# A fifth load buffer, fewer key-value products and a new order in a retention and feed-forward kernel

## The chip, the cores and the metric

The kernel runs on one core of a Trainium2 chip. The metric is the device time of one execution in microseconds (us); less is better. The time of a kernel is the median of several runs.

## The reference

The inputs are `q`, `k` and `v` of shape (8, 8, 576, 64): 8 batches, 8 heads, 576 tokens, 64 elements. First comes a causal retention (attention without a softmax, with a decay for each head), then a feed-forward layer on the 4608 tokens with their heads side by side.

```python
scores = scale * np.matmul(q, k.transpose(0, 1, 3, 2))
gamma = 1.0 - 2.0 ** (-5.0 - np.arange(H, dtype=np.float32))
rel = pos[:, None] - pos[None, :]
Dmat = np.where(rel >= 0, gamma[:, None, None] ** rel[None, :, :], 0.0)
attn = np.matmul(scores * Dmat[None, :, :, :], v)
x = attn.transpose(0, 2, 1, 3).reshape(B * S, H * D)      # 4608 x 512
h = x @ w_in                                              # 512 x 2048
out = np.maximum(0.01 * h, h) @ w_out                     # 2048 x 512, fp32 out
```

## The kernel before

**Units.** The 4608 tokens go in 36 units of 128 (`u`), each two halves of 64 tokens (`j`). A batch has 576 / 64 = 9 halves (`CB`), so batches begin and end in the middle of units. The ninth half of a batch is its last: `live(u, j)` is false there, since no later token of the batch needs its key-value state; `fresh(u, j)` marks a batch's first half.

**Retention of a unit.** `load` (L856) brings k, q and v as fp32, one buffer each from a ring (`ld_pool`, `CFG["ld"]` deep). `casts` (L883) turns k into fp16 (`ck`) and q and v into fp16 with their decay (`cq`, `cv`). q and k are turned around by TensorE (`turn_pe`, units 0 to 7) or by a transposing DMA on SyncE's queue (`turn_dma`, later). `inner` (L962) computes with 64x64 matmuls the scores of each half (`sa`, L973) and the key-value products of each half (`sb`, L982), both into one PSUM tile; VectorE masks the scores (`mk`, L988) and adds the products to the running fp32 state (`st`, L1031 to L1038; tile `s32`), which is cast to fp16 (`sx`, L1051 and L1054; tile `st16`). `outer_mm` (L1092) multiplies scores with values and states with queries (L1096), and `outer_copy` (L1140) copies the outcome into `xT`, the feed-forward layer's input. From unit 13 on the small matmuls of a unit are one burst (`bu`); for units 4 to 11 they are three parts (`sb`, `ca`, `ow`).

**Feed-forward.** Groups of 512 tokens (`g`, nine of them). Groups 0 to 2 use a plain first layer (`layer1`, L1201); groups 3 to 8 use seven products instead of eight on 2x2 blocks (`layer1_set`, L1382), with sums of blocks made by VectorE; the second layer does so in all groups (`layer2`, L1465). ScalarE applies the activation (L1208, L1405, L1414); copies of PSUM between products (`cA`, `u2`, `k5`) run on ScalarE or VectorE, as a list says.

**The order.** Nothing is scheduled by the compiler. Every step is a job with an engine, a modelled cost, what it comes after, and the buffers that it opens and uses. `Plan.order` (L121) plays the jobs through: each engine takes, of the jobs that can start within a slack, the one with the least latest start. That comes from due times of the main stages, the modelled costs of what follows, and two tables of corrections for single jobs, `nudge` and `shift_due`. A third table, `eng`, with five strings of letters for the default, says which engine does a step. The instructions of each engine are then written in the order found. DMAs are modelled as two servers, SyncE's and GpSimd's. GpSimd issues the loads of units 0 to 11 and of both weights in one fixed order, in the same queue as its own casts and scalings; SyncE issues the loads of later units, the transposes and the stores.

**Fillers.** Where the plan shows a gap on TensorE of some length ahead of 60 us, `filler` (L1559) puts matmuls of a zeroed tile there (L1574); `fill_tight` is the time until which short gaps are filled too.

Of the kernel before, what the change touches and what calls it, by code (L numbers as in the profile page):

```python
# [9 lines left out]
FP = mybir.dt.float32  # L10
F16 = mybir.dt.float16
# [36 lines left out]
class Plan:  # L48
# [72 lines left out]
    def order(self, margin=30, slack=30, filler=None):  # L121
# [57 lines left out]
        while todo:  # L179
# [76 lines left out]
def _cfg():  # L256
# [40 lines left out]
    nudge = {  # L297
        -125060:
            "b1.p2.1 ",
        -12876:  # L300
            "so3.1 ",
        -129001:
            "b1.p4.1 ",
        -135715:
            "b1.21 ",
        -137832:
            "b1.11 ",
        -149466:
            "b2.p4.1 ",
        -1547:  # L310
            "mk25 ",
        -15631:
            "b3.p5.0 ",
        -15982:
            "mk27 ",
        -166028:
            "m3.3.0 ",
        -168918:
            "tp5.1 ",
        -18270:  # L320
            "a7.0.p7.0 ",
        -19132:
            "bu32 ",
        -224663:
            "wm1.1 ",
        -2292:
            "m5.2.1 ",
        -239388:
            "wm0.1 ",
        -23999:  # L330
            "b4.p6.1 ",
        -241662:
            "ws3.1 ",
        -25911:
            "ck33 ",
        -2823:
            "b3.p7.1 ",
        -283444:
            "h1.8.256 ",
        -284183:  # L340
            "b0.11 ",
        -289278:
            "ws3.0 ",
        -291604:
            "h1.10.256 ",
        -292799:
            "h1.4.256 ",
        -292880:
            "h1.14.256 ",
        -293315:  # L350
            "b1.p1.1 ",
        -295060:
            "h2.12.0 ",
        -296205:
            "m0.2.0 ",
        -296904:
            "h1.0.0 ",
        -296915:
            "h1.2.0 ",
        -297398:  # L360
            "wm3.1 ",
        -298104:
            "h1.6.0 ",
        -298106:
            "h1.4.0 ",
        -298370:
            "h1.2.256 ",
        -298539:
            "m0.0.1 ",
        -299439:  # L370
            "tp3.1 ",
# [1312 lines left out]
```

## Time and profile before

| | |
|---|---|
| median of 3 runs | 288.48 us (288.45 to 289.79) |
| the profiled execution | 286.13 us, span 284.1 us |
| granted TensorE clock | 0.999 |
| busy, of the span | TensorE 274.5, VectorE 221.9, ScalarE 182.2, GpSimd 92.9 us |
| HBM | read 36.81 MB, written 9.44 MB |
| DMA | 50.06 MB, mean 176 GB/s |

The span is from the first to the last instruction of the profiled execution; the time of the whole execution lies 2.0 us above it. In lines of the profile PE is TensorE's matmuls, PEld its weight loads, DVE VectorE, ACT ScalarE, POOL GpSimd, SP SyncE, and a trailing q the engine's queue. `L982` is line 982 of the kernel. A group's row has the engine, the instruction, out<-in, the shape and count, then the busy time in us, the mean of one in ns, and after a bar the idle time ahead of it with what ended it. Matmuls overlap in the array, so the duration of one is longer than the step from one to the next.

### The profile page before, as it was taken

How to read it: one execution, taken by the hardware profiler on the slowest of the kernel's cores; microseconds unless marked ns; L12 is line 12 of the kernel's file. 1: busy time of each engine (PE TensorE's matmuls, PEld its weight loads, DVE VectorE, ACT ScalarE, POOL GpSimd, SP SyncE). 2: the span in 40 equal slices, each digit the busy share in tenths (PEclk: the TensorE clock that was granted, in tenths of full speed). 3: DMA queues.
4: the chain of work that ended last, by engine and by line, in shares of the span. 5: the costliest groups of instructions: out<-in, count | busy, mean ns of one | idle time of the engine just before them, and what ended most of it. 6: DMA issues, size and time to landing. Idle time of an engine off the chain costs nothing.

```text
span 284.1 us, 10441 instructions
## 1 busy us (share of the span) xinstructions
PE 274.5 (97%) x4530; PEld 231.8 (82%) x4530; DVE 221.9 (78%) x394; ACT 182.2 (64%) x373; POOL 92.9 (33%) x109
## 2 busy tenths in 40 slices
PE   8989899999999999999999999999999999999994
PEld 3668787887788888888888878888888888888883
DVE  3775899865888699898969889889897876955762
ACT  2366576676579598768767766877656755755720
POOL 8888987910122311337324134522100000000000
PEclk9999999999999999999999999999999999999999
DMA  7999999999999999999999999990312002100304
GB/s 158 290 262 237 275 183 284 320 217 228 273 234 194 226 231 272 202 225 240 225 224 212 230 215 229 248 229 0 76 47 105 2 2 76 75 0 3 148 2 148
DMA packets 118797, 50.06 MB, mean 176 GB/s; under 512 B 107488, under 2 KB 112224, under 8 KB 118752
## 3 DMA queue, kind: packets, MB, share of 16 engines
q1 hardware_dynamic: 110368, 35.82, 55.6%
q0 software_dynamic: 7056, 13.11, 19.2%
q8 instruction: 35, 0.57, 0.8%
q10 hardware_dynamic: 1328, 0.47, 0.6%
q14 instruction: 10, 0.08, 0.1%
HBM read 36.81 MB, written 9.44 MB: 163 GB/s over the span
## 4 chain that ended last, share of the span: by engine, by line
PE 82%; DVE 7%; DMA 5%; issue 2%; POOL 2%; ACT 0%; DVEq 0%; POOLq 0%; ACTq 0%
PE acc L1465 38%; PE acc L1382 26%; PE acc L1201 10%; PE ot L1096 4%; DMA w_in<-in_moe_w_in_dram 3%; DMA qkT<-qk 2%; PE sc L982 2%; PE sc L973 2%; POOL t L865 1%; DVE mix L1441 1%; DVE sum L1409 1%; PE acc L938 1%; DVE v L896 1%; DVE s L1037 1%; DVE s L988 1%
## 5 line engine op out<-in xcount | busy, mean ns | idle before, releaser
L1465 PEld LDWEIGHTS <-gt 128*128 128x128 f16 x720 | 69.6, 98 | 8.9 <-ACT gt L1405 0.3
L1465 PE MATMUL acc<-w_out,gt 128*128 128x256 f16 x432 | 54.4, 273 | 0.1
L1201 PE MATMUL acc<-xT,w_in 128*128 128x128 f16 (+1 forms) x512 | 47.1, 246 | 0.5 <-issue 0.5
L1201 PEld LDWEIGHTS <-w_in 128*128 128x128 f16 x512 | 39.1, 98 | 4.4 <-issue 0.7
L1382 PEld LDWEIGHTS <-w_in 128*128 128x128 f16 x384 | 36.8, 98 | 5.5 <-issue 0.8
L1414 ACT ACTIVATE gt<-sum 128x512 f16<-128x512 f32 x48 | 29.8, 629 | 17.8 <-DVE sum L1409 17.7
L1208 ACT ACTIVATE gt<-acc 128x512 f16<-128x512 f32 x48 | 27.8, 594 | 19.9 <-PE acc L1201 19.7
L1405 ACT ACTIVATE gt<-acc 128x512 f16<-128x512 f32 x48 | 28.6, 595 | 14.5 <-PE acc L1382 14.0
L896 POOL TENSOR_TENSOR qk<-t,cs 128x512 f16<-128x512 f32 x19 | 20.6, 1090 | 50.7 <-PE sc L982 22.1
L1465 PE MATMUL acc<-w_mix,gt 128*128 128x256 f16 x288 | 36.4, 273 | 0.0
L1465 PEld LDWEIGHTS <-mix 128*128 128x128 f16 x288 | 27.7, 98 | 4.0 <-DVE mix L1441 0.5
L1382 PEld LDWEIGHTS <-w_sum 128*128 128x128 f16 x288 | 27.6, 98 | 3.9 <-DVE xs L1362 0.4
L1382 PE MATMUL acc<-xs,w_in 128*128 128x256 f16 x192 | 28.8, 273 | 0.7 <-DVE sum L1409 0.7
L1382 PE MATMUL acc<-xs,w_sum 128*128 128x256 f16 x192 | 28.8, 273 | 0.1
L1382 PE MATMUL acc<-xT,w_in 128*128 128x256 f16 x192 | 28.8, 272 | 0.0
L896 POOL TENSOR_TENSOR v<-t,cs 128x512 f16<-128x512 f32 x18 | 20.3, 1127 | 23.7 <-PE ot L1096 19.5
L988 DVE TENSOR_TENSOR s<-sc,cs 128x512 f16<-128x512 f32 x36 | 24.6, 682 | 1.4 <-PE sc L973 1.4
L1335 ACT COPY k<-acc 128x512 f32<-128x512 f32 x27 | 15.9, 591 | 14.2 <-PE acc L1382 7.9
L1409 DVE TENSOR_TENSOR sum<-acc,k 128x512 f32<-128x512 f32 x24 | 16.5, 689 | 7.8 <-ACT k L1335 4.1
L1033 DVE TENSOR_TENSOR s<-sc,s 128x256 f32<-128x256 f32 x40 | 16.7, 418 | 4.1 <-PE sc L982 3.4
L1327 ACT COPY acc<-acc 128x512 f32<-128x512 f32 x30 | 17.4, 579 | 3.1 <-PE acc L1465 1.8
L1096 PE MATMUL ot<-qkT,st 64*64 64x64 f16 x512 | 17.1, 198 | 1.7 <-ACT st L1051 0.5
(68 smaller groups left out, 463.0 us busy)
## 6 DMA issues: line engine op xcount, KB each, us to landing
out_dram<-osb SPq DMA_DIRECT2D x17, 512.0 KB, 4.1
t<-in_k_dram SPq DMA_DIRECT2D x22, 256.0 KB, 4.3
t<-in_q_dram SPq DMA_DIRECT2D x21, 256.0 KB, 4.6
t<-in_v_dram SPq DMA_DIRECT2D x21, 256.0 KB, 4.3
t<-in_v_dram POOLq DMA_DIRECT2D x11, 256.0 KB, 5.5
t<-in_k_dram POOLq DMA_DIRECT2D x10, 256.0 KB, 6.9
t<-in_q_dram POOLq DMA_DIRECT2D x10, 256.0 KB, 6.1
w_in<-in_moe_w_in_dram POOLq DMA_DIRECT2D x8, 256.0 KB, 6.9
```

The costliest lines, as they stand in the source:

```text
L896: engine[e].tensor_tensor(out=out, in0=t32[u, 2 * x][:], in1=decay(u, x), op=MUL)
L988: landed[u] = nc.vector.tensor_tensor(out=s[:], in0=a[:, :, 0], in1=mask_sb.unsqueeze(1).unsqueeze(1).to_broadcast([P, 2, NP, CH]), op=MUL,)
L1033: nc.vector.tensor_tensor(out=to, in0=x, in1=before[0][:, before[1]], op=ADD)
L1096: i = nc.tensor.matmul(out=ot[half(oo), (j + u) % 2, slot, c, :], lhsT=lhsT, rhs=rhs, start=(first or parted(u)) and (j, oo) not in seen, ...
L1201: nc.tensor.matmul(out=a[:, n, :], lhsT=w_in16[:, c, (f0 + n) * P : (f0 + n + 1) * P], rhs=x[:, c, t0 : t0 + nt], start=(n == 0 and c == 0 ...
L1208: nc.scalar.activation(out=y[:, f0 : f0 + nf, t0 : t0 + nt], in_=a[:], func=mybir.ActivationFunctionType.Lrelu)
L1327: op("cA", ce, lambda: copies[ce](out=B[:], in_=A[:]), [done["1"]], [B], [A], "1", COST[ce, "seed"])
L1382: nc.tensor.matmul(out=r[:, f, :], lhsT=w[:, c, (2 * n + f) * P : (2 * n + f + 1) * P], rhs=rhs[:, c, :], start=fresh and c == 0 and f == ...
L1405: w = op(what, "ACT", lambda: nc.scalar.activation(out=to(), in_=r[:], func=lr), after, [y], [r], m)
L1409: what, "DVE", lambda: nc.vector.tensor_tensor(out=s[:], in0=r[:], in1=plus[:], op=ADD),
L1414: lambda: nc.scalar.activation(out=to(), in_=s[:], func=lr), [j], [y], [s],
L1465: nc.tensor.matmul(out=r[:, tb, :], lhsT=lhs[n]()[:, f, tb * P : (tb + 1) * P], rhs=rhs[n][:, f, :], start=fresh and i == 0 and k == 0, st ...
```

## The change

Three things in the kernel and its plan. The ring of load buffers goes from four to five, and the fp32 states `s32` get a ring of their own, of two, where they had one of four. `sb` leaves out the products of a half that is not `live`. The planner's model changes in places: the cost of a burst follows from its number of matmuls, transfers of the two DMA servers hold each other up in another way, and the first quarter of the output weights is costed longer; fillers are put into gaps from 300 ns (before 350) and by that rule until 45 us (before 24). With that, the tables `eng`, `nudge` and `shift_due` are made anew, so the order of instructions and the engine of many steps differ throughout. The list of loads, the strings of letters and the stages stay as they were. The tables of corrections are cut here.

```diff
--- before.py
+++ after.py
@@ -228,11 +228,12 @@
                     at = max(at, server["SP"] + 370, server["POOL"] + 650)
                     server["SP"], land = at + j.move, 170
                 elif j.eng == "SP":
-                    both = min(j.move, max(0.0, server["POOL"] - at))
-                    server["SP"] = at + j.move + 0.5 * both
-                    server["POOL"] += 0.6 * both
+                    if server["POOL"] > at:
+                        at = server["POOL"]
+                        server["POOL"] += 0.1 * j.move
+                    server["SP"] = at + j.move
                 else:
-                    server["POOL"] = at + j.move + 0.5 * min(j.move, max(0.0, server["SP"] - at))
+                    server["POOL"] = at + j.move + 0.1 * min(j.move, max(0.0, server["SP"] - at))
                 j.end = server[j.eng] + land
                 if j.land is not None:
                     j.end = j.land
@@ -282,423 +283,378 @@
     ]
     eng = {
         "ACT":
-            "yt0.0 sx0.0 sx0.1 yt2.1 sx2.1 yt3.1 sx3.0 sx3.1 yt4.0 sx6 sx7 cq8 cq11 cv11 sx10 sx11 cq13 sx12 "
-            "cq16 cv17 sx17 cq18 cv18 cq20 sx21 sx28 ",
+            "yt0.1 sx0.0 sx0.1 yt1.1 sx2.0 sx3.1 cq4 cv5 sx5 cv7 sx7 cq8 cv9 cv10 sx12 sx13 cq17 cq18 sx19 "
+            "cq21 sx30 sx31 sx32 ",
         "DVE":
-            "ck0 cq0 cv0 ck1 cv1 x0 yt1.0 sx1.1 sx2.0 ck4 ck5 yt4.1 yt5.0 yt7.1 x7 ck8 x8 x9 x11 cq12 cv12 "
-            "ck13 cq14 cv14 x13 sx15 ck17 sx16 ck18 x16 sx19 ck20 ck21 cq21 cv21 sx20 x20 cv25 sx24 ck30 ck31 "
-            "x28 x29 sx31 ck32 x31 sx33 ck34 cq34 x32 sx34 sx35 x34 x35 b0.11 b0.u2 b1.u2 a3.3.k5 b2.u2 "
-            "a4.2.u2 a4.3.cA b3.u2 a5.1.u2 b5.k5 a7.1.u2 a7.2.u2 a7.3.k5 b6.u2 b6.k5 a8.1.cA a8.2.u2 b7.u2 "
-            "b7.k5 b8.cA b8.u2 b8.k5 ",
+            "cq0 cv1 ck2 ck3 sx3.0 x3 ck5 x4 yt5.0 ck7 yt6.1 yt7.1 x7 x9 x11 cq12 cq13 cv13 cq15 x12 x15 ck19 "
+            "x16 x17 cq20 x19 x21 ck24 cq25 cv25 x23 sx25 ck27 sx27 cq28 cv28 cq30 x28 x29 x35 b0.11 b0.u2 "
+            "b0.k5 b1.cA b1.k5 a3.2.u2 a4.1.u2 a4.1.k5 a4.2.cA a4.2.u2 a5.2.u2 a6.2.u2 a7.0.u2 a7.3.cA "
+            "a7.3.k5 b6.u2 b6.k5 a8.1.cA a8.2.u2 b7.u2 b7.k5 b8.cA b8.u2 ",
         "POOL":
-            "cq2 ck3 sx4 sx5 cv7 cv8 ck9 sx8 cq10 cv10 ck11 sx13 sx14 cq19 sx18 ck23 sx22 ck24 ck25 ck27 cv29 "
-            "cv30 cv32 cv33 cv34 ck35 ",
+            "sx1.1 cv2 cv8 sx9 cq10 ck12 ck15 ck16 cv16 cv17 ck18 cq19 sx18 sx21 ck22 ck25 sx24 ck26 ck28 "
+            "ck29 cq29 cv29 sx28 sx29 ck30 cv30 ck31 cv31 ck32 cv32 cv33 sx33 ck34 ck35 cv35 ",
     }
     nudge = {
...
     shift_due = {
...
     eng, nudge, shift_due = ({n: v for v, ns in d.items() for n in ns.split()} for d in (eng, nudge, shift_due))
     return dict(
         main=main, engines=engines, loads=loads, eng=eng, nudge=nudge, shift_due=shift_due,
         split=lambda u: u < 4,
-        ld=4, ap=4, t0=7000, extra=1300, l_late=3000, margin=120, slack=60, fill_until=60000, fill_tight=24000,
+        ld=5, ap=4, t0=7000, extra=1300, l_late=3000, margin=120, slack=60, fill_until=60000, fill_tight=45000,
         sp_after=2, period=27000, wm_due=45000, ws_due=30000,
         landing={"ld0.1": 4100, "ld0.0": 4800, "ld0.2": 6700, "wi0": 10500}, u2=("DVE", "DVE"), joined=12,
         drain=4, plain1=(2,), plain2=(), chain=True, order="1265734", shift=8000, tail="1526374", lead=-2000,
@@ -772,6 +728,7 @@
     ld_pool = pool("ld", CFG["ld"])
     a_pool = pool("ap", CFG["ap"])
     b_pool = pool("bp", 2)
+    c_pool = pool("cp", 2)
     d_pool = pool("dp", 2)
     e_pool = pool("ep", 3)
     x_pool = pool("xp", 2)
@@ -826,7 +783,6 @@
         ("ACT", "f32"): (537, 680),
     }
     add = plan.add
-    BURST = 562
 
     def by(name, default):
         return CFG["eng"].get(name, default)
@@ -953,6 +909,9 @@
     def fresh(u, j):
         return (2 * u + j) % CB == 0
 
+    def states(u):
+        return 4 * (2 - fresh(u, 0) - fresh(u, 1))
+
     def st_before(u, j):
         return st16[u][:, 0] if j else st16[u - 1][:, 1]
 
@@ -963,7 +922,7 @@
 
         a = Buf(sc_pool, [P, 2, 2, NP, CH], FP, "sc", True, turn=u)
         s = s16[u] = Buf(b_pool, [P, 2, NP, CH], F16, "s16", turn=u)
-        f, h = Buf(a_pool, [P, 2, NP, CH], FP, "s32", turn=u), Buf(a_pool, [P, 2, NP, CH], F16, "st16", turn=u)
+        f, h = Buf(c_pool, [P, 2, NP, CH], FP, "s32", turn=u), Buf(a_pool, [P, 2, NP, CH], F16, "st16", turn=u)
         s32[u], st16[u] = f, h
 
         def sa():
@@ -978,11 +937,13 @@
         def sb():
             for p in range(NP):
                 for j in range(2):
-                    for g in range(2):
+                    for g in range(2 if live(u, j) else 0):
                         nc.tensor.matmul(
                             out=a[half(g), j, 1, p, :], lhsT=qk16[u][half(j), u % 2, 1, 2 * p + g, :],
                             rhs=v16[u][half(j), 2 * p + g, :], start=True, stop=True, skip_group_check=True,
                         )
+
+        lives = 8 * (live(u, 0) + live(u, 1))
 
         def mk():
             landed[u] = nc.vector.tensor_tensor(
@@ -1003,16 +964,18 @@
                 sa()
                 sb()
 
+            pairs = 32 + lives + states(u - 1) + (states(u - 2) if cross is not None else 0)
+            burst = 31 + 8.3 * pairs
             ja = jb = add(
-                f"bu{u}", "PE", (BURST, BURST + 268), all_,
+                f"bu{u}", "PE", (burst, burst + 268), all_,
                 [turned[u, 0], turned[u, 1], cast[u, 1], cast[u, 2], written.get(u - 2)] + after, [a],
                 [qkT[u], qk16[u], v16[u]] + uses + (cross[1] if cross is not None else []), mode="q",
             )
         elif parted(u):
-            jb = add(f"sb{u}", "PE", (147, 376), sb, [cast[u, 1], cast[u, 2]], [a], [qk16[u], v16[u]], mode="q")
+            jb = add(f"sb{u}", "PE", (14 + 8.3 * lives, 243 + 8.3 * lives), sb, [cast[u, 1], cast[u, 2]], [a], [qk16[u], v16[u]], mode="q")
         else:
             ja = add(f"sa{u}", "PE", (147, 376), sa, [turned[u, 0], turned[u, 1]], [a], [qkT[u]], mode="q")
-            jb = add(f"sb{u}", "PE", (147, 376), sb, [cast[u, 1], cast[u, 2]], [a], [qk16[u], v16[u]], mode="q")
+            jb = add(f"sb{u}", "PE", (14 + 8.3 * lives, 243 + 8.3 * lives), sb, [cast[u, 1], cast[u, 2]], [a], [qk16[u], v16[u]], mode="q")
         if not parted(u):
             masked[u] = add(f"mk{u}", "DVE", COST["DVE", "psum"], mk, [ja], [s], [a])
         if u - 2 >= CFG["joined"]:
@@ -1184,7 +1147,7 @@
                 in_=moe_w_out[c * FQ : (c + 1) * FQ, :].rearrange("(c k) f -> k c f", k=P),
             )
 
-        w_out_job[c] = add(f"wo{c}", "POOL", (770, 770), run, move=2600, due=load_due("POOL"))
+        w_out_job[c] = add(f"wo{c}", "POOL", (770, 770), run, move=3400 if c == 0 else 2600, due=load_due("POOL"))
         follow(w_out_job[c])
 
     leaks = {g: [] for g in range(NG)}
@@ -1558,7 +1521,7 @@
 
     def filler(free, t):
         early = t < CFG["fill_tight"]
-        if t - free < (350 if early else 500) or t > CFG["fill_until"]:
+        if t - free < (300 if early else 500) or t > CFG["fill_until"]:
             return None
         a = Buf(acc_pool, [P, 1, TOK], FP, "acc", True)
         if free < WARM:
```

More of the change, by code (lines that the diff above doesn't have):

```diff
@@ L318, in _cfg @@
[L318 to L367, printed above, removed]
@@ new lines, in _cfg @@
+        -338987:
+            "so0.0 ",
+        -34656:
+            "sx3.0 ",
+        -35084:
+            "b4.p5.0 ",
+        -3564:
+            "b2.p1.1 ",
+        -36122:
+            "mk30 ",
+        -36124:
+            "x28 ",
+        -36392:
+            "tp3.0 ",
+        -375040:
+            "wm3.1 ",
+        -40345:
+            "bu29 ",
+        -42864:
+            "x32 ",
+        -44830:
+            "x21 ",
+        -45449:
+            "b8.p1.1 ",
+        -51461:
+            "st20.1 ",
@@ new lines, in _cfg @@
+        17340:
+            "b3.p1.0 ",
+        20148:
+            "ck20 ",
+        23507:
+            "st32.1 ",
+        24613:
+            "st28.1 ",
+        251269:
+            "cv6 ",
+        25933:
+            "oa35 ",
+        26568:
+            "ld8.1 ",
+        29552:
+            "xs5.3 ",
+        2977:
+            "st18.0 ",
+        30156:
+            "bu35 ",
+        32293:
+            "b4.p3.0 ",
+        3550:
+            "ck24 ",
+        42319:
+            "b5.p4.0 ",
```

596 lines of the change are left out of this document (275 added, 321 removed).

## The prediction, made before the change was run

> **What bounds the kernel now.** I read the page first, then the busy time by stretches, then TensorE's own groups, waits and timeline, and last the queues of GpSimd and SyncE.
>
> ```profile
> PE 274.5 (97%) x4530; PEld 231.8 (82%) x4530; DVE 221.9 (78%) x394; ACT 182.2 (64%) x373; POOL 92.9 (33%) x109
> ...
> PE 82%; DVE 7%; DMA 5%; issue 2%; POOL 2%; ACT 0%; DVEq 0%; POOLq 0%; ACTq 0%
> ```
>
> The first line is the page's busy times, the second its chain of work that ended last. Both name TensorE. An average hides stages, so here are five stretches, each with the busy time of every engine, the clock and the DMA share:
>
> ```profile
> core 0: us, PE busy (x) PEld busy (x) DVE busy (x) ACT busy (x) POOL busy (x), PEclk, DMA share, GB/s
> 0.00:30.00 30.00, 26.48 (x482) 17.51 (x482) 16.96 (x37) 14.04 (x26) 25.99 (x37) 1.00 1.01 239
> 30.00:60.00 30.00, 29.20 (x538) 25.14 (x537) 28.13 (x44) 19.45 (x46) 25.01 (x30) 1.00 1.09 262
> 60.00:190.00 130.00, 128.65 (x2387) 110.59 (x2385) 109.22 (x198) 96.17 (x208) 37.59 (x38) 1.00 1.07 228
> 190.00:270.00 80.00, 79.81 (x1039) 69.80 (x1037) 61.75 (x107) 50.79 (x93) 4.34 (x6) 1.00 0.16 54
> 270.00:284.10 14.10, 10.32 (x94) 8.80 (x91) 5.87 (x10) 1.74 (x4) 0.00 (x0) 0.99 0.21 76
> ```
>
> From 30 to 270 us TensorE sits idle for 0.80 + 1.35 + 0.19 = 2.34 us in 240. So in the long middle the end moves only by work taken off TensorE, or by those 2.34 us. The first 30 us are another regime: 3.52 us idle, GpSimd busy 25.99 of 30 and the DMA share at 1.01. And the busy time there is not all useful, because some of it is matmuls on a zeroed tile that the planner puts into gaps. The next two rows are TensorE's group of those, and the record of the key-value products that the change cuts:
>
> ```profile
> L1574 PE MATMUL acc<-idle 128*128 128x512 f16 x34 | 11.6, 461 | 1.6 <-DVE idle L808 1.2 <-issue 0.4
> ```
> ```profile
> L982 PE MATMUL sc<-v,qk x576: 186/193/214, 7.6 to 226.2; 64*64 64x64 f16 x192
> ```
>
> So 34 fillers take 11.6 us, all of it ahead of 30 us; the slot in which a start could be better is there. TensorE's waits, total us, times, longest:
>
> ```profile
> PE acc L1382 <- DVE sum L1409: 0.7, 1, 0.7
> PE sc L982 <- issue: 0.6, 1, 0.6
> PE acc L1201 <- issue: 0.5, 1, 0.5
> PE ot L1096 <- ACT st L1051: 0.5, 1, 0.5
> ```
>
> No wait occurs twice; there is no systematic stall to remove, only single ones that an order may miss or make.
>
> **The products left out.** Per unit of 128 tokens there are 576 / 36 = 16 products at L982. Eight halves of units, one per batch, end a batch; each loses 8 products, 64 in all. What one costs is not its 193 ns latency but its pitch. Three rows of TensorE's timeline (start, us):
>
> ```profile
> 102.30 0.32 PE L973 MATMUL sc<-qkT 64*64 64x64 f16 x16
> 102.44 0.34 PE L982 MATMUL sc<-v,qk 64*64 64x64 f16 x16
> 102.71 1.05 PE L1465 MATMUL acc<-w_mix,gt 128*128 128x256 f16 x8
> ```
>
> Sixteen small matmuls take 102.44 - 102.30 = 0.14 us, 8.75 ns each; the last sixteen take 0.27 us until full-size work starts, so 0.13 us is the change of tile size, which stays. 64 x 8.75 ns = 0.56 us is the most this can save. The least is about nothing: the shapes say 64*64, so four of these products may run at a time on the quarters of the array; one half of a unit uses two of the quarters, and eight products there are four deep, as sixteen were on four. I take 0.4 us, nearer to the row, because the short products just ahead can overlap with the empty quarters. The Trainium skill (TensorEngine Tiling (Array Packing), Key Properties) says that different tiles load weights and multiply in parallel; by that rule, four rounds stay four rounds, and the saving would be 0. The row of 8.75 ns agrees that quarters overlap, and nothing in this trace shows eight products on two quarters, so which end holds is open.
>
> **The fifth load buffer, and the ring of two.** With four buffers the first load that SyncE issues in the middle (unit 12) needs the slot of unit 8. SyncE's own waits:
>
> ```profile
> SPq L865 <- DVE qk L892: 32.6, 2, 32.3
> ```
>
> That is 32.3 us behind a key cast, which I read as unit 8's. With five it needs unit 7's cast, and may issue some microseconds sooner. Bytes do not change, and from 30 to 190 us the DMA share is 1.07 to 1.09, so transfers begun sooner share the same engines. I cost it at 0 by itself: what it gives is room for the order, and its cover is that none of the TensorE waits shown is for a load. The room comes from the fp32 states, whose ring goes from four to two: a state update on VectorE must then wait until the cast of the state two units back has read it, with VectorE's queue behind it and TensorE behind that. Units follow each other by (226.2 - 7.6) / 35 = 6.2 us on average, two units by 12, and a cast takes under 1 us (rows below). Cost 0; if a cast is queued late on GpSimd, up to its own length, 0.8 us, each time.
>
> **Engines.** The order is remade, and with it 138 small steps change engine. Counted from the lists: VectorE loses 12 full casts and 4 scalings, and gains 4 copies; GpSimd gains 9 full casts and 4 scalings and loses one half cast; ScalarE stays about level. Groups of GpSimd, and one of VectorE:
>
> ```profile
> L896 POOL TENSOR_TENSOR qk<-t,cs 128x512 f16<-128x512 f32 x19 | 20.6, 1090 | 50.7 <-PE sc L982 22.1 <-issue 10.5 <-ACT acc L1327 7.0
> L896 POOL TENSOR_TENSOR v<-t,cs 128x512 f16<-128x512 f32 x18 | 20.3, 1127 | 23.7 <-PE ot L1096 19.5 <-ACT gt L1208 4.2
> ...
> L892 POOL CAST qk<-t 128x512 f16<-128x512 f32 x8 | 5.0, 636 | 0.6 <-DMA t<-in_k_dram 0.6
> L1051 POOL CAST st<-s 128x512 f16<-128x512 f32 x6 | 5.0, 828 | 20.4 <-DVE s L1033 14.0 <-DVE s L1037 5.1 <-ACT gt L1208 1.1
> ...
> L1054 POOL CAST st<-s 128x256 f16<-128x256 f32 x5 | 3.0, 605 | 9.1 <-DVE s L1037 6.8 <-DVE s L1031 2.3
> ```
> ```profile
> L892 DVE CAST qk<-t 128x512 f16<-128x512 f32 x14 | 6.8, 494 | 8.0 <-DMA t<-in_k_dram 5.3 <-ACT gt L1208 1.8 <-PE sc L982 0.9
> ```
> ```profile
> L896 DVE TENSOR_TENSOR v<-t,cs x15: 679/684/1531, 6.8 to 209.0; 128x512 f16<-128x512 f32 x15
> ```
>
> VectorE: 12 x 0.494 + 4 x 0.68 - 4 x at most 0.69 = about 5.9 us less of 221.9. GpSimd: 9 x 0.64 to 0.83 + 4 x 1.1 - 0.6 = 9.5 to 11.3 us more of 92.9. Neither is on the path as a sum, since from 60 us on GpSimd is busy 37.59 of 130 us and VectorE 109.22. It counts at the single waits: 0.7 of the 2.34 us is a wait for VectorE. From 30 to 60 us, VectorE is busy 28.13 of 30, so a relief there is worth most.
>
> **The order itself.** The trace of before can't show the new one, so I bound it. Best in the middle: all 2.34 us gone. I take half, 1.1. In the first 30 us, the fillers from 11.65 us on are these, the first and the last of six groups with 14 matmuls:
>
> ```profile
> 11.65 0.81 PE L1574 MATMUL acc<-idle 128*128 128x512 f16 x3
> ...
> 29.49 0.60 PE L1574 MATMUL acc<-idle 128*128 128x512 f16 x2
> ```
>
> One more matmul adds 0.81 - 0.60 = 0.21 us, so 14 hold about 3 us; all of the idle time ahead of 30 us is 3.52. Much of this waits on weights and loads, which come no sooner, as the list of loads is the same. I take 0.7 us of gain, at best 1.8, at worst a loss (the second rival). The filler rule is also loosened (gaps of 300 ns instead of 350, and the tight rule up to 45 us instead of 24): a filler that lands on ready work costs up to 0.21 us, five of them 1 us, taken inside the 0.7. The number of returns from small to full-size matmuls, 0.13 us each, I keep equal.
>
> **Sum.** 0.4 + 1.1 + 0.7 = 2.2 us. The profiled execution took 286.13 us, its span 284.1 and 2.0 around it; that gives 283.9 for a like execution. The median of the runs, 288.48, lies 2.35 above the profiled one, and I keep that: 288.48 - 2.2 = 286.3 us. The best is 0.56 + 2.34 + 1.8 = 4.7 us less, 283.8.
>
> **The rivals.** First, nothing comes of the order: the new one misses the old single waits and makes others of the same size, and only the products show, 288.48 - 0.4 = 288.1 us. For it: the middle holds 1% of idle time, and 9.5 to 11.3 us more GpSimd work shares the memory with VectorE. A pair that ran together, GpSimd's and VectorE's timelines:
>
> ```profile
> 57.79 1.04 POOL L896 TENSOR_TENSOR v<-t,cs 128x512 f16<-128x512 f32 x1
> ```
> ```profile
> 57.89 1.49 DVE L896 TENSOR_TENSOR v<-t,cs 128x512 f16<-128x512 f32 x1
> ```
>
> VectorE's took 1.49 us against a median of 0.684, so it seems to have stood still for 0.8 us. If 7 of the 13 added GpSimd steps catch such a VectorE step, 7 x 0.8 = 5.6 us eat the relief of 5.9. The Trainium skill (GPSIMD Engine Reference, Specifications) says that GpSimd shares its memory interfaces with VectorE and contends with VectorE instructions of two memory inputs; the pair agrees. Against it: the old order carries such clashes too and yet leaves 2.34 us.
>
> Second, slower: GpSimd's queue in the first 24 us. It issues the loads of both weights and inputs, in order, and its steps run in the same queue:
>
> ```profile
> 10.49 0.75 POOL L1175 DMA_DIRECT2D w_in<-in_moe_w_in_dram x1 [0.94 <-DMA w_in<-in_moe_w_in_dram]
> ...
> 13.98 1.08 POOL L896 TENSOR_TENSOR qk<-t,cs 128x512 f16<-128x512 f32 x1
> ...
> 22.99 0.62 POOL L1175 DMA_DIRECT2D w_in<-in_moe_w_in_dram x1 [0.35 <-DMA w_in<-in_moe_w_in_dram]
> ```
>
> For units 0 to 3 it gets the value scalings of 0 and 2 and two half casts, 2 x 1.127 + 2 x 0.605 = 3.5 us, and is rid of one scaling and one cast, 1.09 + 0.64 = 1.7. A step that waits for its load or its state blocks every issue behind it, the input weights among them, and the layer-one blocks behind those. The delay of the whole start is 1.8 us net, 3.5 if all four stand ahead of the weights and what is removed stood behind; the middle is 2.6, less 0.4: 288.48 + 2.2 = 290.7. It decides when the eighth issue of the input weights, at 22.99 us now, falls after 25 us. Against it: waits of 0.94 and 0.35 us in that queue, which would absorb part.
>
> That the change doesn't do what it says can be left aside for the products, whose loop is cut in plain sight.
>
> **How the numbers follow.** About 0.5% or 1.44 us is what a measurement of this kernel can tell. Forecast 286.3 us, chance 0.52, own range 283.8 to 287.0, all faster by over 0.5%. No net gain, 288.1: 0.25, all within 0.5%. Slower by the queue, 290.7 (289.9 to 291.9): 0.23. The range from 283.8 to 290.8 leaves out the upper half of the last case and a little below the best, under 2 in 10.
>
> **What would show it.** The products: 512 instead of 576 at L982, and the gap from them to full-size work in an end-of-batch unit 0.04 to 0.07 us shorter than 0.27. The start: TensorE's busy time without fillers in the first 30 us above 26.48 - 11.6 = 14.9 us, and fewer than 34 fillers. The middle: idle from 30 to 270 us near 1.2 us. VectorE's busy sum near 216, GpSimd's near 103. SyncE's first middle load ahead of unit 8's key cast. I am wrong if the input weights' last issue is past 25 us, if VectorE's sum doesn't fall, or if new waits of TensorE above 1 us stand in the middle.

## The result and the profile after

The change makes the kernel slower: 290.56 us median (288.71 to 292.02, 14 runs) against 288.47 us for the kernel before (286.79 to 290.6, 14 runs), a ratio of 1.0072, 95% interval 1.0046 to 1.0098. Forecast were 286.3 us and "faster". Here and below a median is of all runs, while a ratio leaves out runs over 1.5% above the fastest of their kernel, so that it need not be the quotient of two medians. The profiled execution after took 291.1 us (span 289.3), that of before 286.13 us (span 284.1). The spans differ by 5.2 us, the medians by 2.1, since the profile of before lies 2.3 us below its median and that of after 0.5 above. So the trace shows where this execution lost its 5.2 us, and not all of that is the change's.

The page's busy times, the busy times by the same five stretches as before, and TensorE's waits, all of the kernel after:

```profile
PE 276.0 (95%) x4463; PEld 234.0 (81%) x4463; DVE 223.3 (77%) x382; ACT 182.6 (63%) x373; POOL 103.8 (36%) x121
```
```profile
core 0: us, PE busy (x) PEld busy (x) DVE busy (x) ACT busy (x) POOL busy (x), PEclk, DMA share, GB/s
0.00:30.00 30.00, 25.41 (x411) 17.68 (x412) 13.62 (x26) 13.41 (x27) 25.69 (x37) 0.89 1.00 219
30.00:60.00 30.00, 27.31 (x504) 23.47 (x502) 28.85 (x44) 22.76 (x63) 23.34 (x26) 1.00 1.11 270
60.00:190.00 130.00, 128.07 (x2339) 109.49 (x2337) 112.42 (x199) 85.88 (x176) 45.21 (x49) 1.00 1.05 226
190.00:270.00 80.00, 79.81 (x1082) 70.07 (x1080) 59.52 (x102) 54.67 (x100) 9.58 (x11) 1.00 0.18 55
270.00:289.30 19.30, 15.41 (x140) 13.26 (x137) 8.91 (x14) 5.92 (x12) 0.00 (x0) 0.96 0.22 83
```
```profile
PE acc L894 <- DVE qk L852: 1.8, 3, 0.9
...
PE sc L932 <- DVE qkT L901: 0.9, 1, 0.9
PE acc L894 <- DVE qk L848: 0.9, 1, 0.9
PE acc L1345 <- DVE u L1295: 0.9, 1, 0.9
PE acc L1345 <- DVE sum L1372: 0.7, 2, 0.5
```

TensorE's idle time by stretch is now 4.59, 2.69, 1.93, 0.19 and 3.89 us, where it was 3.52, 0.80, 1.35, 0.19 and 3.78. Nearly all the loss lies ahead of 60 us. The waits ahead of 60 us are nearly all for VectorE, on the small steps of retention (scaling, key cast, copy of the turned tile), each under 1 us. The clock column has 0.89 in the first row, a cost that shows as busy time. Split further (same columns), and with the instructions around it on TensorE, VectorE and GpSimd:

```profile
15.00:17.50 2.50, 1.58 (x39) 0.86 (x38) 2.47 (x5) 1.25 (x3) 1.51 (x2) 1.00 1.17 248
17.50:20.00 2.50, 1.46 (x40) 1.33 (x41) 1.69 (x5) 0.41 (x1) 2.39 (x4) 0.58 1.14 244
20.00:22.50 2.50, 2.50 (x27) 2.50 (x24) 1.37 (x4) 0.60 (x1) 1.45 (x3) 0.50 1.17 237
22.50:25.00 2.50, 2.38 (x51) 2.00 (x50) 0.48 (x1) 1.18 (x2) 2.06 (x4) 0.55 0.69 202
```
```profile
17.94 0.43 PE L932 MATMUL sc<-qkT 64*64 64x64 f16 x16 [0.93 <-DVE qkT L901]
18.17 0.40 PE L941 MATMUL sc<-v,qk 64*64 64x64 f16 x16
19.18 3.60 PE L1164 MATMUL acc<-xT,w_in 128*128 128x128 f16 x32 [0.60 <-issue]
```
```profile
16.24 1.30 DVE L1000 TENSOR_TENSOR s<-stmp,cs 128x256 f32<-128x256 f32 x1
17.47 0.41 DVE L901 COPY qkT<-acc 128x512 f16<-128x512 f16 x1
```
```profile
16.23 1.04 POOL L852 TENSOR_TENSOR v<-t,cs 128x512 f16<-128x512 f32 x1 [0.76 <-DMA t<-in_v_dram]
```

This is one chain. Unit 2's value scaling, now on GpSimd, begins at 16.23; VectorE's state update at 16.24 takes 1.30 us, where the same update takes 0.42 at 31.57 us. The copy behind it is late, TensorE pauses for 0.93 and 0.60 us, and the granted clock goes to 0.50 to 0.58 for seven microseconds: 32 matmuls of layer one take 3.60 us, where as many take 1.96 at 27.62 us. Over the 14 runs of after the clock was 0.985 to 0.998, under 0.995 in 12 of them, so a fall of some size is usual. In the span's sum for this execution: idle +3.0 us ahead of 60 us and +0.7 behind, about 2.6 us of busy time from the cold clock, and as the remainder 1.1 us less of other busy time (fewer fillers and products among it), 5.2 in all.

### The profile page after: what moved, and what is told of

Same layout as the page of the kernel before. It is cut to its first block, busy times and chain, and to the rows that moved or that the text cites. A ratio compares the mean times of both kernels' runs of the same rounds, so it can differ in the third digit from the quotient of the medians.

```text
span 289.3 us, 10303 instructions
## 1 busy us (share of the span) xinstructions
PE 276.0 (95%) x4463; PEld 234.0 (81%) x4463; DVE 223.3 (77%) x382; ACT 182.6 (63%) x373; POOL 103.8 (36%) x121
## 4 chain that ended last, share of the span: by engine, by line
PE 80%; DVE 12%; DMA 3%; POOL 2%; issue 2%; ACT 0%; DVEq 0%; POOLq 0%
PE acc L1428 36%; PE acc L1345 24%; PE acc L1164 13%; PE ot L1059 4%; DMA t<-in_q_dram 3%; PE sc L932 2%; POOL t L821 2%; PE sc L941 2%; DVE w_mix L1212 1%; DVE qk L852 1%; DVE sum L1372 1%; DVE s L1000 1%; DVE s L949 1%; DVE w_sum L1241 1%; DVE s L996 1%
## 5 line engine op out<-in xcount | busy, mean ns | idle before, releaser
L1164 PE MATMUL acc<-xT,w_in 128*128 128x128 f16 (+1 forms) x512 | 49.3, 254 | 1.1 <-issue 0.6
L1164 PEld LDWEIGHTS <-w_in 128*128 128x128 f16 x512 | 40.7, 102 | 5.1 <-issue 1.2
L1345 PEld LDWEIGHTS <-w_in 128*128 128x128 f16 x384 | 37.0, 98 | 6.1 <-issue 1.2
L852 POOL TENSOR_TENSOR v<-t,cs 128x512 f16<-128x512 f32 x23 | 27.6, 1203 | 24.7 <-PE ot L1059 16.5
L852 POOL TENSOR_TENSOR qk<-t,cs 128x512 f16<-128x512 f32 x18 | 19.7, 1101 | 38.6 <-PE sc L941 26.5
L1014 POOL CAST st<-s 128x512 f16<-128x512 f32 x9 | 6.4, 706 | 37.3 <-DVE s L996 28.5
L1290 ACT COPY acc<-acc 128x512 f32<-128x512 f32 x28 | 16.1, 576 | 4.8 <-PE acc L1345 2.3
```

The source lines that it names most:

```text
L852: engine[e].tensor_tensor(out=out, in0=t32[u, 2 * x][:], in1=decay(u, x), op=MUL)
L1164: nc.tensor.matmul(out=a[:, n, :], lhsT=w_in16[:, c, (f0 + n) * P : (f0 + n + 1) * P], rhs=x[:, c, t0 : t0 + nt], start=(n == 0 and c == 0 ...
L1290: op("cA", ce, lambda: copies[ce](out=B[:], in_=A[:]), [done["1"]], [B], [A], "1", COST[ce, "seed"])
L1345: nc.tensor.matmul(out=r[:, f, :], lhsT=w[:, c, (2 * n + f) * P : (2 * n + f + 1) * P], rhs=rhs[:, c, :], start=fresh and c == 0 and f == ...
```

## The experiments

Unless said otherwise, each kernel is the changed one with one edit, in its own order, and each ratio is to the kernel before on the same chip, with the 95% interval. Theories in short: A, the cold clock; B, later G, the late start behind GpSimd's queue; C, VectorE held up by GpSimd's steps; D, the engines chosen; E, the new order itself; F, the early loads of the fifth buffer.

**e1_fill**: eight idle matmuls more where the clock fell, five in a gap and three in front of a layer-one block.

```
+FILLS, FILL_NO = {7: 6}, [0]                    # the seventh gap: 6 instead of 1
...
+    for _ in range(3 if (g, f0, t0) == (0, 4, 0) else 0):
+        nc.tensor.matmul(out=a[:]..., lhsT=idle[:, 0:P], rhs=idle, start=True, stop=True)
```

> The changed kernel with 5 more idle matmuls at 16.6 us and 3 ahead of the layer-one block at 19.2 us; nothing else moves. Theory A (clock): in the changed kernel TensorE has pauses of 0.93 and 0.60 us between 17.0 and 19.2 us, and behind them the granted clock is 0.50 to 0.58 from 17.5 to 25 us; of the 5.2 us that the span is longer, 2 to 2.6 us are this. It expects the clock near 0.999 and 287.9 to 288.9 us (ratio to before 0.998 to 1.002). Theory B (the queue of GpSimd: value scaling of unit 0 runs there behind load issues, the start is 2.8 us late) and theory C (VectorE held up by GpSimd steps from 34 to 41 us) both expect no gain from this: ratio 1.006 to 1.008, as the work behind the pauses is late anyway.

Measured: 291.19 us, 1.0101 (1.0076 to 1.0127). The clock of its profile is 0.998 and TensorE's work at 41 us stands 3 us further than in after, yet the end is no earlier. Among its waits are new ones, the first for the turned tile of a DMA, the others for the output weights:

```profile
PE sc L933 <- DMA qkT<-qk: 1.0, 1, 1.0
...
PE acc L1431 <- DVE w_mix L1215: 0.6, 1, 0.6
...
PE acc L1431 <- DMA w_out<-in_moe_w_out_dram: 0.3, 1, 0.3
```

The clock alone is not the cause: what it gives is spent waiting further on. It is worth something all the same. Over the 151 runs that the ratios use of the fourteen kernels with the new order and its engines, those with a clock under 0.995 take on average 0.5 us (0.1 to 0.9) more than the other runs of the same kernel. Such a clock stands in 12 of after's 14 runs and in 21 of 144 runs of before beside the experiments; an estimate from these numbers puts about 0.4 of the 2.1 us down to it.

**e2_cv2, e3_cv0, e4_cq67**: single early steps taken off GpSimd: unit 2's value scaling (behind its turned-tile copy), unit 0's (with six fillers instead of twelve ahead of it), and the query scalings of units 6 and 7.

```
+RUN_ON = {'cv2': 'DVE'}      # e2
+RUN_ON = {'cv0': 'DVE'}      # e3
+RUN_ON = {'cq6': 'DVE', 'cq7': 'DVE'}      # e4
```

> The changed kernel with the value scaling of unit 2 run on VectorE, behind its copy of that unit's turned keys, instead of on GpSimd; the rest of the order stays. The scaling at 16.23 us on GpSimd runs beside a state update on VectorE that takes 1.30 us instead of 0.42, and TensorE waits 0.93 us for the copy behind it. If that clash starts the clock's fall (A, by way of C): update 0.42 us, wait under 0.2 us, clock 0.998 or more, ratio 0.998 to 1.003. If the pause at 19.2 us alone is enough for the fall, or B holds: wait gone but clock as before, ratio 1.004 to 1.008.

> The changed kernel with the value scaling of unit 0 run on VectorE instead of on GpSimd, and 6 idle matmuls instead of 12 in the gap that it leaves at 7.1 us. Theory B: first key-value products at 8.7 instead of 10.1 us, first layer-one block at about 12 instead of 13.4, and the end 1.4 us earlier, ratio 1.001 to 1.003. Theories A and C: the start is earlier but TensorE waits for loads and weights further on, end within 0.5 us, ratio 1.005 to 1.009.

> The changed kernel with the query scalings of units 6 and 7 run on VectorE instead of on GpSimd, at their place in the order. Theory C: VectorE's steps at 35.8 and 37.6 us (1.26 and 2.33 us) come down to 0.5 and 0.7, TensorE's waits for VectorE between 36 and 41 us fall from 2.3 to under 1 us, end 1.3 us earlier, ratio 1.001 to 1.004. Rival (VectorE is full there anyway, and GpSimd's load issues hold it, not its scalings): two more steps of 0.7 us on VectorE, waits as before or longer, ratio 1.006 to 1.010.

Measured: 1.0059 (1.0019 to 1.0099), 1.0078 (1.0040 to 1.0116) and 1.0075 (1.0037 to 1.0113). Each did its local work: in e2 the update takes 0.42 us again, a pause of 0.35 us stands where one of 0.93 was, and the clock is 1.000 in the profile (under 0.995 still in 7 of the 12 runs); in e3 the first products come at 8.78 us instead of 10.11; in e4 the waits of 36 to 41 us shrink to 0.5 us and less. None moves the end by what can be told from after.

**e5_engines, e6_engines**: after's order with before's engines for the 138 steps, and the reverse, before's order with after's engines (buffers and products of before).

```
+RUN_ON = {'ck0': 'DVE', 'cv0': 'DVE', 'x0': 'DVE', ...      # 138 names
```

> The changed kernel's order, with each of the 138 steps that changed engine run where it ran before the change, at its place in the new order. Theory D (engines): the new choice of engines costs, since GpSimd steps hold up VectorE's; GpSimd's sum falls from 104 to about 93 us, and the ratio to before from 1.007 to 0.997 to 1.002. Theory E (order): the places of loads, weights and blocks in the new order cost, whichever engine does the small steps; ratio 1.005 to 1.015, the more as the order was not made for these engines. Theory F (fifth buffer: unit 12's loads start 8 us sooner on SyncE's queue and slow the output weights): ratio 1.004 to 1.010, as those loads stay where they are.

> The reverse: the order of before, with each of the 138 steps run on the engine that the change gives it, at its place in the old order; four load buffers, all products. Theory D: GpSimd's sum rises from 93 to about 104 us, VectorE's does not fall in spite of 12 fewer casts, ratio 1.005 to 1.010. Theory E: the old order keeps its time, 0.998 to 1.004. Theory F: as E. A mismatch of order and engines alone would cost in this and in the last run alike, by 0.5% or more each.

Measured: 295.55 us, 1.0245 (1.020 to 1.029), and 293.65 us, 1.0204 (1.016 to 1.0247). Both mixtures are far slower than either kernel: an order and its engines are made for each other, and the two theories can't be parted this way.

**e7_rings and e8_products**: the kernel before with one part of the change, in the old order: five load buffers and a ring of two; the 64 products left out.

```
-    ld_pool = pool("ld", CFG["ld"])             # e7
+    ld_pool = pool("ld", 5)
+    c_pool = pool("cp", 2)                      # and s32 opens in it
-                    for g in range(2):          # e8
+                    for g in range(2 if live(u, j) else 0):
```

> The kernel before with five load buffers and a ring of two for the fp32 states, the order of every instruction as before. Theory F: SyncE's first loads of unit 12 start at about 42 instead of 50.8 us and take over 10 instead of 5 us, the last output weights land 2 us or more later, ratio 1.003 to 1.008. Theories D and E: 0.998 to 1.002, no new wait on VectorE from the ring of two.

> The kernel before with the 64 key-value products of the last halves left out, the order otherwise as before. All theories: a gain of 0 to 0.56 us, 0.4 us as predicted, ratio 0.998 to 1.000, too small for the interval; the timeline tells it: the step from the products to full-size work in a late end-of-batch unit 0.20 to 0.24 us instead of 0.27.

Measured: e7 288.86 us, 1.0026 (0.9997 to 1.0055); e8 286.99 us, 0.9957 (0.9925 to 0.9988). e8 beats both kernels. Its 1.2 us are more than the 0.56 that the products can save by the prediction's row; where the rest comes from is not shown. No wait for the ring of two shows in e7's trace.

**e9_hold, e10_queue, e11_both**: unit 12's loads held until the first mix of the output weights; four early steps off GpSimd with fillers moved; and both.

```
+    if (u, x) == (12, 1): tc.add_manual_dep(i.ins, first_mix[0].ins.name, ...)      # e9, e11
+RUN_ON = {'cv0': 'DVE', 'cv2': 'DVE', 'sx1.1': 'ACT', 'sx2.1': 'ACT'}               # e10, e11
```

> The changed kernel with SyncE's loads of unit 12 and all behind them held until VectorE's first mix of the output weights (at about 50 us; 42.3 us in the changed kernel). Theory F (these early loads, which the fifth buffer allows, slow the output weights): the slowest output weight lands in under 11.5 us instead of 12.7, unit 12's loads in 5 to 8 us instead of 18, ratio 1.001 to 1.005. Rivals G (GpSimd's queue is late from the start) and E (order): ratio 1.006 to 1.010, since TensorE is not waiting for the output weights in the changed kernel, and the loads behind unit 12 come later.

> The changed kernel with the four early steps taken off GpSimd's queue (value scalings of units 0 and 2 to VectorE, two half casts to ScalarE), and idle matmuls moved so that TensorE has no pause over 0.5 us ahead of 20 us. Theory G (GpSimd's queue): the last issue of the input weights at 22 to 23 us instead of 24.6, the first of the output weights at 32 instead of 33.7, bytes moved in the first 30 us back from 6.57 to over 6.9 MB, clock 0.998 or more, ratio 1.000 to 1.004. Rival F: the start is earlier, then TensorE waits 1 to 2 us for output weights from 48 to 58 us, ratio 1.004 to 1.009. Rival E (the order further on): the same ratio without these waits.

> Both of the last two in one: four early steps off GpSimd's queue, idle matmuls moved, unit 12's loads held. If F and G are two walls one behind the other, this alone comes down: ratio 0.995 to 1.001, with no wait for output weights over 0.5 us. If the order further on (E) is what costs, 1.003 to 1.009, with idle time of TensorE from 60 to 190 us at 2 us or more as in the changed kernel (1.93; 1.35 before).

Measured: 1.0032 (1.0005 to 1.0058), 1.0054 (1.0021 to 1.0088), 1.0054 (1.0021 to 1.0086). All three kept the clock in their profiles (1.000, 1.000 and 0.998; under 0.995 in 3, 5 and 7 of 12 runs) and stayed slower than before. Holding the loads brought 0.4% from after to e9, but nothing from e10 to e11. TensorE's waits in e9:

```profile
PE sc L938 <- DMA qkT<-qk: 1.9, 2, 1.5
...
PE acc L1351 <- DVE u L1301: 0.9, 1, 0.9
PE acc L1351 <- DVE sum L1378: 0.7, 2, 0.5
```

The first is the transpose of units 18 and 19, at 117 us, which does not show in after, where TensorE arrives later; the others stand at 132 us as in after.

**e12_products**: the changed kernel with all 576 products, `for g in range(2):`.

> The changed kernel with the 64 key-value products put back, all else as in the changed kernel. In the order of before leaving them out gave a ratio of 0.9957 (0.9925 to 0.9988). If they are worth the same here, this one comes to 1.010 to 1.013 to before, and order, engines and rings alone cost that. If the gain of the products was partly a luckier start in that run, 1.007 to 1.010.

Measured: 1.0056 (1.0023 to 1.0090). Cutting the products is worth nothing that can be told in the new order.

**e13_late, e14_late_hold, e15_late_both**: the two late waits taken away, in after, on top of e9, and on top of e11. Steps are moved behind a named one in the written order:

```
+    for name in ("so1.0", "ld22.1", "ld21.2", "ld21.0"):
+        behind(name, "tr18")                    # the transpose of units 18, 19
+    behind("m3.2.0", "a3.2.u2")                 # a mix behind the copy
```

> Two steps of the changed order moved at two places past 100 us, all else as after: on SyncE the transpose of units 18 and 19 goes ahead of three loads and one store that stood before it (it was issued at 109.61 in after, its last input being ready at about 107.2), and on VectorE one copy of a layer-one block goes ahead of one of the mixes (TensorE waited 0.9 us for that copy at 132 us in after, 11% of nothing else). Theory E (the loss is a handful of places in the new order, in series): TensorE's wait at 132 us falls from 0.9 to about 0.3, the transpose is not what after waits for, so 0.5 to 0.7 us in all, ratio to before 1.004 to 1.006. Rival (the loads' stream sets the pace, and a wait taken away returns at the next transpose or load): the waits move by under 0.3 us in sum, ratio as after's, 1.007.

> The two moves of e13_late, and the early loads of unit 12 held as in e9_hold, where TensorE waited 1.9 us for that transpose at 117 us and 0.9 us for that copy. Theory E: both waits go, 1.9 + 0.6 = 2.5 us off the 289.3 of e9_hold, about 286.8, ratio 0.993 to 0.998, faster than before. Rival (stream): at least half of the 1.9 us comes back at the transpose of units 20 and 21 or 22 and 23, with loads issued later in their place; ratio 1.001 to 1.004.

> The two moves of e13_late on top of e11_both (early loads held, four early steps taken off GpSimd's queue, the idle matmuls moved), where TensorE waited 1.0 us for the transpose and 0.9 us for the copy. Theory E: 1.0 + 0.6 us off its 290.2, about 288.6, ratio 0.999 to 1.001. Rival (stream): the transpose's wait returns later, ratio 1.003 to 1.006.

Measured: 290.85 us, 1.0043 (1.0000 to 1.0086); 290.44 us, 1.0057 (1.0019 to 1.0095); 291.51 us, 1.0082 (1.0045 to 1.0119). The first is inconclusive, the other two go against theory E as I had put it, a handful of misplaced steps. TensorE's waits from 60 to 190 us in e14:

```profile
PE acc L1351 <- DVE sum L1378: 1.4, 2, 1.2
PE acc L1351 <- ACT osb L1467: 0.9, 1, 0.9
PE acc L1351 <- DVE u L1301: 0.3, 1, 0.3
```

The wait for the transpose is gone and the copy's fell from 0.9 to 0.3 as meant, but the sum behind it in VectorE's queue went from 0.7 to 1.4, and a wait for an output copy is new. In this run VectorE is late at that place as a queue: moving its jobs changed which of them TensorE waits for. Holding the loads brought nothing here either, from e13 to e14.

**e16_no_order, e17_four, e18_order_alone**: so the question was put by parts. e16 is before with everything but the order (e7 and e8 together); e17 is after with four load buffers; e18 also has all products.

```
+    ld_pool = pool("ld", 4)                     # e17, e18; the order stays
+                    for g in range(2):          # e18
```

> Every part of the change but the order and its engine choice: the kernel before with its own order and engines, five load buffers, the ring of two and the 64 products left out (e7_rings and e8_products together). If the parts add up, 1.0026 times 0.9957 = 0.9983, about 288.0 us (0.996 to 1.001), and the new order with its engine choice costs after 1.0072 / 0.9983 = 0.9%, some 2.6 us. Rival (the loss sits in the buffers, and the order has nothing to do with it): near after's 1.007, or at least 1.004.

> The changed kernel with the fifth load buffer undone (four, as before), its order, engines, ring of two and products as in after: each load of units 12 and later is issued at the same place of SyncE's queue, but waits for the buffer of the unit four before it. If the early loads of the fifth buffer collide with the weights (e9_hold suggested half of the loss), it comes out at 1.000 to 1.004 and unit 12's loads are issued later than the 42 to 45 us of after; if the order needs the fifth buffer (its due times were made for it), TensorE waits more for transposes and casts from 60 us on, and it is at 1.007 or over; the theory that the order alone is the cause says within 0.002 of after's 1.0072.

> The new order with its engine choice alone (and the ring of two, which no trace shows a wait at): four load buffers, all 576 products. It is the last of the eight ways to have or not have the order, the fifth buffer and the 64 products. The sum of parts fitted to the six changed kernels so far (order +0.36%, buffers +0.38%, products left out -0.12%) says 1.0036, 1.001 to 1.006. The prediction's step for the order (1.1 us from the middle and 0.7 from the first 30 us) says 0.994. If the order costs only together with the fifth buffer's early loads, it is 0.998 to 1.001.

Measured: e16 1.0043 (1.0012 to 1.0075), e17 288.96 us, 1.0027 (0.9990 to 1.0065), e18 289.74 us, 1.0038 (1.0005 to 1.0071). With before as 1, all eight combinations are there:

| order and engines | load buffers | all products | 64 left out |
|---|---|---|---|
| old | four | 1 (before) | 0.9957 (e8) |
| old | five | 1.0026 (e7) | 1.0043 (e16) |
| new | four | 1.0038 (e18) | 1.0027 (e17) |
| new | five | 1.0056 (e12) | 1.0072 (after) |

The new order is the slower one in all four pairs that differ only in it (+0.38, +0.30, +0.70 and +0.29%), five buffers in all four that differ in them (+0.26, +0.86, +0.18 and +0.45%); the products go either way (-0.43, +0.17, -0.11 and +0.16%). A sum of three parts fitted to the seven ratios, weighted by their intervals, gives: new order and engines +0.37% (0.16 to 0.57), fifth buffer +0.38% (0.19 to 0.57), products left out -0.11% (-0.31 to +0.08). The fit takes the ratios as independent, though those of one chip share runs of before. The sum, +0.63%, lies within after's interval. Worst fitted are e8 (fit 0.9989) and e16 (1.0026), in opposite directions. I had expected 0.9983 for e16, and the rival beside it, that the loss sits in the buffers, 1.004 or more; it measured 1.0043. The parts alone don't add up that well, and that the products save more with four buffers than with five is possible but not shown.

Two things are mixed in. The ring of two goes with the fifth buffer in the old order and with the new order otherwise; no trace shows a wait for it, but no run has it alone. And the new order was planned for five buffers, so e17 and e18 run it with a ring that it was not made for.

Where the new order loses shows in one stretch. From 115 to 140 us, before and e18 (same columns as the stretches above):

```profile
115.00:140.00 25.00, 24.96 (x504) 21.65 (x503) 22.60 (x43) 17.82 (x34) 10.20 (x12) 1.00 1.02 227
```
```profile
115.00:140.00 25.00, 22.75 (x422) 19.29 (x422) 19.49 (x35) 17.29 (x32) 10.29 (x12) 1.00 1.03 227
```

TensorE is idle for 0.04 us there in before, e7 and e8, and for 1.5 (after) to 3.3 us in the profiles of all fourteen kernels with the new order and its engines. These are single executions, and that this stretch alone makes the cost is not shown.

What the fifth buffer does first is on SyncE's queue. The start of unit 12's loads in after, and the first in e17:

```profile
42.27 0.38 SPq L821 DMA_DIRECT2D t<-in_k_dram  x1
42.74 0.53 SPq L821 DMA_DIRECT2D t<-in_q_dram  x1
44.79 6.91 SPq L821 DMA_DIRECT2D t<-in_v_dram  x1
```
```profile
50.74 0.38 SPq L822 DMA_DIRECT2D t<-in_k_dram  x1
```

They are issued 8 us earlier, into DMA engines that are full (share 1.11 from 30 to 60 us), and in after take 14 to 18.5 us to land instead of 5.6 to 7.5 in before. In after the first output-weight matmul comes at 48.6 us, the first of these on a sum of activation blocks (`mix`) at 59.2; in e17:

```profile
L1429 PE MATMUL acc<-w_out,gt x79: 269/273/283, 44.6 to 75.0; 128*128 128x256 f16 x79
L1429 PE MATMUL acc<-w_out,mix x16: 272/272/273, 55.2 to 56.8; 128*128 128x256 f16 x16
```

That is four microseconds earlier, but it is not the buffer's doing: in e10, with five buffers and unit 12's first load issued at 37.59 us, the two come at 44.0 and 55.1. e10 and e17 share a start with the clock kept, which the profiled execution of after lacks.

So the eight combinations show that five buffers cost, together with the ring of two in the old order, and by about 0.3%, not clear of noise, without it in the new. Why they cost stays open. e9, which keeps unit 12's loads back by a dependency, agrees with e17 (1.0032 and 1.0027), but the same hold did nothing in e11 and e14, and the output weights landed hardly later (at most 12.7 us from issue in after, 11.9 in e17, 11.8 in before).

## Why the prediction was wrong

**Products: the step shrank, its worth doesn't show.** 512 products run, and the step from them to full-size work shrank. Two bursts of after, an end-of-batch unit and a full one:

```profile
92.30 0.29 PE L941 MATMUL sc<-v,qk 64*64 64x64 f16 x8
92.52 0.72 PE L1164 MATMUL acc<-xT,w_in 128*128 128x256 f16 x5
```
```profile
99.12 0.33 PE L941 MATMUL sc<-v,qk 64*64 64x64 f16 x16
99.39 0.61 PE L1164 MATMUL acc<-xT,w_in 128*128 128x256 f16 x4
```

0.22 against 0.27 us (0.22 to 0.23 in five such units, 0.24 to 0.27 in full ones): eight times about 0.03 us is 0.2 us, where 0.4 was taken. The Trainium skill's rule (TensorEngine Tiling (Array Packing), Key Properties), that different tiles work in parallel, gave 0; these rows lie halfway between. The fit says 0.3 us (-0.2 to 0.9), which leaves all of these values open.

**Fifth buffer: the first failed step.** "I cost it at 0 by itself", since transfers begun sooner share the same engines. The fit's +0.38% is 1.1 us (0.5 to 1.6). By which transfer or wait is not known: that the early loads take from transfers which TensorE needs sooner is one reading, and of the three pairs of runs with and without these loads held, one bears it out. My cover, that no TensorE wait shown is for a load, spoke only of loads at the old times. The sign asked for, SyncE's first middle load earlier, came true (42.27 for 50.77 us), and no gain came with it. The ring of two cost nothing that a trace shows.

**Order: the second failed step, and the one furthest off.** -0.7 us ahead of 30 us and -1.1 in the middle were forecast; the fit gives +1.1 us (0.5 to 1.6), 2.9 us apart. Idle from 30 to 270 us, forecast near 1.2, is 2.69 + 1.93 + 0.19 = 4.8 us; with four buffers it is 4.4 us in e17 and 7.2 in e18, against 2.34 in before. The new order made more and longer waits than it removed. I took half of a bound as the likely value; nothing in the trace of before carried that half. With the buffer's 1.1 the two steps make 4.0 of the 4.3 us between the forecast -2.2 and the measured +2.1.

**Engines: GpSimd's sum right, VectorE's wrong.** GpSimd's 103.8 us is the 103 forecast. VectorE should have fallen to 216 and went from 221.9 to 223.3 with 12 instructions fewer. Two groups of VectorE, before and then after:

```profile
L896 DVE TENSOR_TENSOR qk<-t,cs 128x512 f16<-128x512 f32 x11 | 7.7, 704 | 3.5 <-DMA t<-in_q_dram 1.6 <-PE sc L982 1.5 <-DMA cs<-ret_consts 0.4
L1249 DVE TENSOR_TENSOR w_out<-w_out 128x1024 f16<-128x1024 f16 x2 | 1.4, 688 | 0.0
```
```profile
L852 DVE TENSOR_TENSOR qk<-t,cs 128x512 f16<-128x512 f32 x13 | 11.9, 920 | 5.5 <-DMA cs<-ret_consts 4.0 <-DMA t<-in_q_dram 1.5
L1212 DVE TENSOR_TENSOR w_out<-w_out 128x1024 f16<-128x1024 f16 x2 | 2.4, 1218 | 0.0
```

The same operation's mean rises from 704 to 920 ns and from 688 to 1218, by single long ones: of the two at L1212 one takes 0.69 us, the other 1.74 beside a GpSimd scaling of 1.06. That is the mechanism of the first rival, clashes that eat the relief; here they come to 223.3 - 216 = 7.3 us, where 5.6 were said. That the size came so near is partly luck, for how much it is depends on the timing: other executions with the same VectorE work summed to 218.0 (e9) and 219.0 (e17). The Trainium skill (SBUF - State Buffer, SBUF: two separate sides) says that VectorE's instructions with two inputs in that memory and GpSimd's take turns at a shared pair of ports, each for its whole instruction; the rows agree, 1.30 us for 0.42 beside a GpSimd step of 1.04.

**The slower rival: its number right, its mechanism not shown.** 290.7 us was its time. That the number fits is luck. The eighth issue of the input weights fell at 24.61 us, 1.6 later, near the 1.8 net that I had reckoned, but not past the 25 us that I had set. And this delay doesn't set the time: with four of the steps taken off GpSimd's queue (e10) the issue is back at 23.03 us and the ratio is 1.0054 (1.0021 to 1.0088), not parted from after's; in e17 it falls at 25.02 us and the ratio is 1.0027.

**The signs.** Useful TensorE time ahead of 30 us came out at 25.41 less the fillers' 9.1 us, 16.3, over the 14.9 that I called right. A colder clock lengthens matmuls and passes that sign; less the 2.6 us of it, 13.7 are left, under 14.9. Busy time isn't progress unless the clock stands beside it. Of my three signs of being wrong one came, VectorE's sum that doesn't fall; the waits over 1 us and the issue past 25 us did not.

**What stays open.** The order with its engines costs 0.2 to 0.6%, part of it likely in the stretch from 115 to 140 us, and no single step was found that does it. Waits removed at 18, 40, 117 and 132 us came back elsewhere. TensorE and the DMA engines are both nearly full to about 190 us (128.07 of 130 us busy and a DMA share of 1.05 from 60 us on in after), which would explain that, but no run took load off the DMA to test it. Why the fifth buffer costs is open too.

## What to carry to other kernels

A kernel that keeps one engine 97% busy has little to give to a new order and much to lose: price a remade order by its bounds on both sides, not by half of the better one. A deeper ring of load buffers need not be free when the DMA engines are full; here it cost about 0.4%, for a reason that was not found. When a cure removes its wait and the time stays, stop mending places and run the parts of the change in all combinations; eight kernels said here what ten repairs had not.

## What the runs showed of the hardware

The clock can fall without a long pause. In after, idle times of 0.93 and 0.60 us around light 64x64 matmuls and one filler were followed by a granted clock of 0.50 to 0.58 over 17.5 to 25 us; TensorE was busy for 1.58 of the 2.5 us ahead of that and for 1.46 of the first 2.5 in it. With eight fillers more there (e1) the clock of the first 30 us was 1.00. The Trainium skill (TensorE: Matmul & The Clock Gate, Part 1: The HAM clock gate) has it fall after an idle window of about 3.4 us; here no pause was near that long.
